# Held-back loads, a weight converted by halves, and eight-by-two diagonal blocks on another engine in a fused attention and feed-forward kernel

## The chip, the cores and the metric

One core of a Trainium2 chip runs the whole program. The metric is device time in microseconds (us); lower is better. TensorE (PE) multiplies, VectorE (DVE) and ScalarE (ACT) do elementwise work, GpSimd (POOL) does one kind of reduction and issues transfers, SyncE (SP) only issues transfers. Each engine works through its own queue in order.

## What is computed

```python
# q, k, v: 8 batches x 8 heads x 576 tokens x 64
q_s = softmax(q, over the 64 of a head)
k_s = softmax(k, over the 576 tokens)
kv  = einsum('bhsd,bhse->bhde', k_s, v)          # 64 x 64 for each batch and head
x   = einsum('bhsd,bhde->bhse', q_s, kv)         # -> 4608 tokens x 512
h   = x @ w_in                                   # 512 -> 2048
x   = maximum(0.01 * h, h) @ w_out               # 2048 -> 512
h   = max(x @ w1, x @ w2, x @ w3)                # 512 -> 768, three times
out = h @ w_out2                                 # 768 -> 512
```

The inputs are 64-bit floats for the weights (read as pairs of 32-bit words) and every matmul operand is split into a high and a low part, so that a product takes three matmuls (hi·hi, hi·lo, lo·hi).

## The kernel before, in words

The 4608 tokens are nine chunks of 512. A chunk is first put through the attention and then, transposed, through the first feed-forward layer, whose 2048 hidden columns are 16 blocks (m = 0 to 15); each block has a weight tile (its piece of `w_in` and of `w_out`). The list `TURNS` says in which order chunks 0 and 1 take the blocks while the weights come in: chunk 0 with block 0, chunk 1 with blocks 0 and 1, chunk 0 with blocks 1 to 3, and so on. A step of this loop is one projection (12 matmuls, `project`), the leaky function, a split (`split_g`) and the second product of the step before (12 matmuls, `a_out`).

A planner (the framework's scheduler, with a simulated timeline) orders each engine's instructions when the program is built. It takes what is ready first, and of what is ready the instruction that stands earlier in the program; `pin` ties an instruction behind the one written before it on its engine. So the order of the instructions may change anywhere when something is edited.

The part around the change is the start, before the loop is in its rhythm.

- `first_units(0)` and `first_units(1)` are the attention units of chunks 0 and 1: four pairs of heads, each with a k unit (`kv_unit`, L382) and a q unit (`q_unit`, L500), advanced stage by stage by `advance` (L787). Their k, v and q are loaded by SP into one `spare` tile for each pair (L396, L399, L505).
- The k unit transposes k (L411), takes the maximum (L416 to L418), the exponential (L430, L431, L428), multiplies by v (L455), and writes the two 64x64 diagonal blocks of kv, scaled, into `plain`: a ScalarE copy from PSUM (L465), after two small VectorE instructions (L460, L461).
- The q unit subtracts, exponentiates, sums and scales (L526 to L549), transposes on TensorE (L555) and copies the transpose out of PSUM into a tile `qf` (L557), for which there are three buffers for four pairs of heads; then it multiplies with `plain` (L563) and splits the result (`split_x`: L605 to L615), which is the operand of `project`.
- PSUM has four buffers under the name `ps`, which the transposes, the kv products and the products of L563 take in turn.
- Chunk 2's units are background work of the loop, planned for steps 13 to 21 (`plan_units`, L724); they load through POOL (L396, L445, L505) into tiles of a small pool (two buffers for k and q, one for v). `behind_step` (L366) makes a tile's first column depend on the newest result of the loop, by a ScalarE copy of one column.
- `conv_a(m, after)` (L720) converts the 64-bit weight m into the high and low part by `split_words` (L155): ScalarE takes the absolute value of the whole tile into a single-buffered tile `ca` (L172), VectorE makes seven passes over 1024 columns (L173 to L185), ScalarE writes the high part (L177) and a copy that goes to DRAM (L188, L189). Weight 0 is converted before the loop, weights 1 and 2 in step 0 (L923, L924), the others at the steps in `BEGUN`, two steps after their load (`load_a`).

## Time and profile before

| what | value |
|---|---|
| median of 3 runs | 1414.36 us (1412.64 to 1415.6) |
| the profiled execution | 1412.0 us; its span from first to last instruction 1410.2 us |
| PE busy | 1382.3 us, 98% of the span |
| DVE, ACT, POOL busy | 866.5, 673.7, 157.5 us |
| granted TensorE clock, mean | 0.997 |

All times in the rows are microseconds from the start of the span. An instruction's row gives its start and its duration, and in brackets how long its engine sat idle before it and what ended that. Where a row stands for several instructions (x4), the start is that of the first. Instructions of one engine overlap a little, so the distance between two starts may be shorter than a duration.

### The profile page before, as it was taken

How to read it: one execution, taken by the hardware profiler on the slowest of the kernel's cores; microseconds unless marked ns; L12 is line 12 of the kernel's file. 1: busy time of each engine (PE TensorE's matmuls, PEld its weight loads, DVE VectorE, ACT ScalarE, POOL GpSimd, SP SyncE). 2: the span in 40 equal slices, each digit the busy share in tenths (PEclk: the TensorE clock that was granted, in tenths of full speed). 3: DMA queues.
4: the chain of work that ended last, by engine and by line, in shares of the span. 5: the costliest groups of instructions: out<-in, count | busy, mean ns of one | idle time of the engine just before them, and what ended most of it. 6: DMA issues, size and time to landing. Idle time of an engine off the chain costs nothing.

```text
span 1410.2 us, 18328 instructions
## 1 busy us (share of the span) xinstructions
PE 1382.3 (98%) x6624; PEld 1128.3 (80%) x6624; DVE 866.5 (61%) x1500; ACT 673.7 (48%) x1382; POOL 157.5 (11%) x261
## 2 busy tenths in 40 slices
PE   6999998999999999999999999999999999999998
PEld 4688777788888788888887888888888888888887
DVE  8878888865686794756756545766357255434311
ACT  6756867854675755654444444224224223322211
POOL 1000112210111120210222300011000000000000
PEclk9999999999999999999999999999999999999999
DMA  9478776743986956768698897765574573454601
GB/s 370 152 261 288 254 249 211 231 147 116 355 290 230 397 189 228 282 237 341 215 331 303 297 390 263 250 225 172 199 285 142 209 291 119 155 233 157 229 33 38
DMA packets 90826, 330.10 MB, mean 234 GB/s; under 512 B 10672, under 2 KB 27056, under 8 KB 67568
## 3 DMA queue, kind: packets, MB, share of 16 engines
q1 hardware_dynamic: 68512, 251.46, 49.4%
q0 software_dynamic: 19056, 66.98, 14.1%
q10 hardware_dynamic: 3168, 10.49, 1.9%
q8 instruction: 52, 0.85, 0.2%
q14 instruction: 38, 0.31, 0.1%
HBM read 253.66 MB, written 75.24 MB: 233 GB/s over the span
## 4 chain that ended last, share of the span: by engine, by line
PE 87%; DVE 5%; DMA 4%; ACT 3%; issue 2%; SPq 0%; ACTq 0%; DVEq 0%
PE ps L859 40%; PE acc L631 32%; PE ps L631 11%; DMA outw<-stream_out 1%; PE ps L455 1%; PE ps L583 1%; DMA stream_in<-room 1%; PE ps L563 1%; DMA spare<-in_q_dram 1%; DVE glo L652 1%; DMA room<-wi 0%; DMA lone<-room 0%; DVE side L824 0%; ACT qo L519 0%; DVE qsm L541 0%
## 5 line engine op out<-in xcount | busy, mean ns | idle before, releaser
L859 PE MATMUL ps<-op,group 128*128 128x512 f32 x1512 | 352.2, 389 | 0.0
L859 PEld LDWEIGHTS ps<-op,group 128*128 128x128 f32 x1512 | 283.8, 188 | 59.0 <-ACT snap L1091 0.2
L631 PE MATMUL acc<-ghi,outw 128*128 128x512 f32 x768 | 248.0, 391 | 1.9 <-ACT ghi L651 1.6
L859 PE MATMUL ps<-opA,group 128*128 128x512 f32 x1008 | 247.5, 391 | 1.1 <-ACT opA L819 0.6
L859 PEld LDWEIGHTS ps<-opA,group 128*128 128x128 f32 x1008 | 188.1, 188 | 41.6 <-ACT snap L987 1.4
L631 PEld LDWEIGHTS acc<-ghi,outw 128*128 128x128 f32 x768 | 143.6, 188 | 33.5 <-ACT ghi L651 3.1
L631 PE MATMUL acc<-glo,outw 128*128 128x512 f32 x384 | 150.4, 392 | 0.5 <-DVE glo L652 0.2
L631 PE MATMUL acc<-wo,h 128*128 128x512 f32 x558 | 135.6, 389 | 0.0
L631 PE MATMUL acc<-ghi,w 128*128 128x512 f32 x384 | 127.1, 395 | 0.9 <-ACT ghi L651 0.9
L631 PE MATMUL ps<-xhi,w 128*128 128x512 f32 x384 | 125.7, 394 | 1.0 <-ACT g L909 0.8
L1091 ACT ACTIVATE snap<-ps 128x512 f32<-128x512 f32 x108 | 61.9, 597 | 135.4 <-PE ps L859 135.1
L631 PEld LDWEIGHTS acc<-wo,h 128*128 128x128 f32 x558 | 104.8, 188 | 21.7
L652 DVE TENSOR_TENSOR glo<-g,ghi 128x512 fp32r<-128x512 f32 x102 | 69.9, 691 | 59.8 <-ACT ghi L651 59.3
L1106 DVE TENSOR_TENSOR snap<-snap,ps 128x512 f32<-128x512 f32 x72 | 49.1, 684 | 93.2 <-ACT snap L1091 69.8
L651 ACT ACTIVATE ghi<-g 128x512 fp32r<-128x512 f32 x102 | 63.6, 630 | 46.9 <-DVE g L1291 27.3
L631 PEld LDWEIGHTS ps<-xhi,w 128*128 128x128 f32 x384 | 72.1, 188 | 17.3 <-ACT g L909 1.2
L631 PEld LDWEIGHTS acc<-glo,outw 128*128 128x128 f32 x384 | 72.1, 188 | 17.2 <-DVE glo L652 2.5
L631 PEld LDWEIGHTS acc<-ghi,w 128*128 128x128 f32 x384 | 71.5, 188 | 16.8 <-ACT ghi L651 1.5
L1102 DVE TENSOR_TENSOR best<-snap,ps 128x512 f32<-128x512 f32 x36 | 24.7, 686 | 87.9 <-PE ps L859 37.7
L631 PE MATMUL acc<-glo,w 128*128 128x512 f32 x192 | 75.2, 392 | 0.5 <-DVE glo L652 0.5
L631 PE MATMUL ps<-xlo,w 128*128 128x512 f32 x192 | 75.1, 391 | 0.1
L1115 ACT ACTIVATE h<-best 128x512 fp32r<-128x512 f32 x48 | 30.3, 631 | 87.3 <-DVE best L1108 86.9
(185 smaller groups left out, 1915.6 us busy)
## 6 DMA issues: line engine op xcount, KB each, us to landing
group<-stream SPq DMA_DIRECT2D x62, 1024.0 KB, 6.2
outw<-stream_out SPq DMA_DIRECT2D x48, 1024.0 KB, 8.1
group<-stream_in SPq DMA_DIRECT2D x42, 1024.0 KB, 7.5
stream<-room POOLq DMA_DIRECT2D x66, 256.0 KB, 6.3
raw<-in_wa_dram SPq DMA_DIRECT2D x16, 1024.0 KB, 7.0
x<-st SPq DMA_DIRECT2D x40, 256.0 KB, 3.7
room<-in_wb_dram POOLq DMA_DIRECT2D x18, 512.0 KB, 6.2
stream_out<-w SPq DMA_DIRECT2D x16, 512.0 KB, 3.6
```

The source lines that it names most:

```text
L455: nc.tensor.matmul(acc[z, : D + 1], lhsT=ke[:, r, z], rhs=vt[:, r, h], start=r == 0, stop=r == RK - 1)
L563: nc.tensor.matmul(both(xps, c0, c1), lhsT=plain_of(b, hp), rhs=halves(qf, c0, c1), start=True, stop=True)
L583: nc.tensor.matmul(both(xps, c0, c1), lhsT=a, rhs=halves(y, c0, c1), start=i == 0, stop=i == 2)
L631: nc.tensor.matmul(acc, lhsT=l, rhs=r, start=first and i == 0, stop=last and i == 2)
L651: nc.scalar.activation(hi[:, z], g[:, z], AF.Copy)
L652: nc.vector.tensor_tensor(lo[:, z], g[:, z], hi[:, z].bitcast(F32), op=ALU.subtract)
L859: nc.tensor.matmul(bank, lhsT=l, rhs=r, start=fresh and first, stop=last, skip_group_check=not fresh)
L1091: nc.scalar.activation(t, bank, AF.Copy)
L1102: nc.vector.tensor_tensor(g, snap, bank, op=ALU.add)
L1106: nc.vector.tensor_tensor(snap, snap, bank, op=ALU.add)
L1115: nc.scalar.activation(h[:, m, 0], g, AF.Copy)
```

## The change

It has four parts. In chunk 2, the loads of k for the first two pairs of heads, of q for the same two and of v for the first are put behind a `behind_step`, so that they can't be issued before the step in which they are written. The conversion of weight 1 is a generator with three parts: the absolute value right after step 0's split, the first half of the columns (`w_in`'s piece) once all k units of chunk 1 are done, the second half after the rest of chunk 1's attention; each VectorE and ScalarE pass is over 512 columns instead of 1024. For chunks 0 and 1 the diagonal blocks of `plain` are written by VectorE. And for these chunks the transposed q goes back into the tile that q came from, instead of one of three `qf` buffers.

```diff
+    def split_by_halves(raw, hi, lo, keep):
+
+        words = raw.bitcast(U32).rearrange("p (n t) -> p n t", t=2)
+        a = cp.tile([P, 2 * N], U32, tag="ca", name="ca")
+        pin(nc.scalar.activation(a.bitcast(F32), words[:, :, 1].bitcast(F32), AF.Abs))
+        yield
+        for i in range(2):
+            z = slice(i * N, i * N + N)
+            au, high, low = a[:, z], words[:, z, 1], words[:, z, 0]
+            af, bf = au.bitcast(F32), high.bitcast(F32)
+            pin(nc.vector.tensor_scalar(af, af, MOST_HIGH, LEAST_HIGH, op0=ALU.min, op1=ALU.max))
+            nc.vector.tensor_scalar(au, au, 3, 0x3FFFFFF8, op0=ALU.logical_shift_left, op1=ALU.bitwise_and)
+            nc.vector.scalar_tensor_tensor(au, high, 0xC0000000, au, op0=ALU.bitwise_and, op1=ALU.bitwise_or)
+            nc.scalar.activation(hi[:, z], af, AF.Copy)
+            nc.vector.tensor_scalar(high, au, 0xFF800000, None, op0=ALU.bitwise_and)
+            nc.vector.scalar_tensor_tensor(bf, low, 2.0**-52, bf, op0=ALU.mult, op1=ALU.mult)
+            nc.vector.tensor_tensor(af, af, bf, op=ALU.add)
+            nc.vector.tensor_tensor(lo[:, z], af, hi[:, z].bitcast(F32), op=ALU.subtract)
+            yield
+        copy = raw.bitcast(F32)[:, :N]
+        nc.scalar.activation(copy, a.bitcast(F32)[:, :N], AF.Copy)
+        pin(nc.scalar.dma_start(keep, copy))
...
         fetch = nc.sync if b < FIRST else nc.gpsimd
+        if b == FIRST and hp < 2:
+            behind_step(ke[:, 0, 0:1])
         fetch.dma_start(ke, k[b, hp])
...
+            if b == FIRST and hp == 0:
+                behind_step(vt[:, 0, 0, 0:1])
             fetch.dma_start(vt, v[b, hp])
...
-                nc.scalar.activation(plain_of(b, hp)[z, z], acc[z, :D], AF.Copy, scale=rc[z])
+                if b < FIRST:
+                    nc.vector.tensor_scalar(plain_of(b, hp)[z, z], acc[z, :D], rc[z], None, op0=ALU.mult)
+                else:
+                    nc.scalar.activation(plain_of(b, hp)[z, z], acc[z, :D], AF.Copy, scale=rc[z])
...
+        if c == FIRST and hp < 2:
+            behind_step(qt[:, 0:1])
         (nc.sync if c < FIRST else nc.gpsimd).dma_start(qt, q[c, hp])
...
-        qf = ap.tile([P, N], F32, tag=("qf", "qhi", "qlo")[hp % 3] if early else "qf", name="qf", bufs=1)
+        if c < FIRST:
+            qf = qt
+        else:
+            qf = ap.tile([P, N], F32, tag=("qf", "qhi", "qlo")[hp % 3] if early else "qf", name="qf", bufs=1)
...
     def conv_a(m, after):
         tiles[m] = weights(words.pop(m), after, whole_in[m])
+        wA[m] = parts(tiles[m])
+
+    def conv_by_halves(m):
+        raw = words.pop(m)
+        if raw.dtype != I64:
+            yield
+            yield
+            tiles[m] = weights(raw, None, whole_in[m])
+        else:
+            w = tiles[m] = wp.tile([P, 2, 2, N], F32R, tag="w", name="w")
+            yield from split_by_halves(raw, flat(w[:, 0]), flat(w[:, 1]), whole_in[m])
         wA[m] = parts(tiles[m])
...
             newest["g"] = g
+            if step == 0:
+                convert = conv_by_halves(1)
+                next(convert)
             background(step)
             if prev is not None:
                 a_out(*prev)
...
                 second = advance(second, 2)
                 a_out(*prev, hold=True)
                 prev = None
+                while len(done) < 2 * NP:
+                    second = advance(second, 1)
+                next(convert)
                 advance(second)
+                for _ in convert:
+                    pass
                 for f in range(KDM):
                     store(f, x2[turn][:, f], accs[c][f], busy=True)
-                conv_a(1, spare(1, NP - 1))
                 conv_a(2, x_tiles(1)[0][:, NP - 1].bitcast(F32))
```

## Rows read from the trace of the kernel before

**Rows 1.** The page's first part: busy time, share of the span and instructions of each engine.

```profile
PE 1382.3 (98%) x6624; PEld 1128.3 (80%) x6624; DVE 866.5 (61%) x1500; ACT 673.7 (48%) x1382; POOL 157.5 (11%) x261
```

**Rows 2.** One of TensorE's waits, whole run: for what, us in total, times, longest.

```profile
PE ps L455 <- DMA vt<-in_v_dram: 2.3, 1, 2.3
```

**Rows 3.** Stretches: busy us (count) of PE, PEld, DVE, ACT, POOL; clock, DMA share, GB/s.

```profile
10.00:20.00 10.00, 6.76 (x32) 5.21 (x31) 8.68 (x26) 7.36 (x17) 0.00 (x0) 0.83 1.03 405
...
120.00:140.00 20.00, 20.00 (x90) 16.54 (x90) 18.35 (x25) 13.11 (x22) 1.48 (x1) 1.00 0.84 297
```

**Rows 4.** Transfers of 0 to 70 us issued by POOL: count, KB each, us to landing.

```profile
ke<-in_k_dram POOLq DMA_DIRECT2D x2, 320.0 KB, 7.6
qt<-in_q_dram POOLq DMA_DIRECT2D x2, 256.0 KB, 8.5
vt<-in_v_dram POOLq DMA_DIRECT2D x1, 325.0 KB, 9.1
```

**Rows 5.** The same view of 8.0 to 8.6 us: the load of weight 0.

```profile
raw<-in_wa_dram SPq DMA_DIRECT2D x1, 1024.0 KB, 11.8
```

**Rows 6.** The chain that ended last (start, us, what): chunk 0's last q; a later second product.

```profile
4.01 8.65 DMA spare<-in_q_dram
...
73.63 2.72 PE acc L631 x12
```

**Rows 7.** VectorE in order of time, 0 to 80 us: start, us, instruction.

```profile
7.25 0.69 DVE L526 TENSOR_REDUCE qmx<-spare 128x8 f32<-128x512 f32 x1 [0.99 <-DMA spare<-in_q_dram]
...
12.68 0.69 DVE L526 TENSOR_REDUCE qmx<-spare 128x8 f32<-128x512 f32 x1 [1.28 <-DMA spare<-in_q_dram]
...
22.07 0.69 DVE L173 TENSOR_SCALAR ca<-ca 128x1024 f32<-128x1024 f32 x1 [1.69 <-ACT ca L172]
...
33.96 0.69 DVE L541 TENSOR_REDUCE qsm<-spare 128x8 f32<-128x512 f32 x1 [0.57 <-ACT spare L539]
...
45.35 1.54 DVE L427 TENSOR_TENSOR spare<-spare,ps 128x640 f32<-128x640 f32 x2
```

**Rows 8.** ScalarE in order of time, 0 to 80 us.

```profile
14.00 0.63 ACT L539 ACTIVATE spare<-spare 128x512 f32<-128x512 f32 x1 [1.54 <-DVE spare L538]
...
20.88 1.16 ACT L172 ACTIVATE ca<-raw 128x1024 f32<-128x1024 f32 x1
...
25.88 1.94 ACT L465 ACTIVATE plain<-ps,rc 64x64 f32<-64x64 f32 x6
...
48.55 1.14 ACT L172 ACTIVATE ca<-raw 128x1024 f32<-128x1024 f32 x1
...
51.68 0.60 ACT L557 ACTIVATE qf<-ps 128x512 f32<-128x512 f32 x1
```

**Rows 9.** TensorE in order of time, 0 to 120 us.

```profile
46.37 2.79 PE L455 MATMUL ps<-spare 128*64 128x65 f32 x80
50.40 4.17 PE L563 MATMUL ps<-qf,plain 128*128 128x64 f32 x16 [1.25 <-ACT plain L465]
...
56.52 0.50 PE L631 MATMUL ps<-xhi,w 128*128 128x512 f32 x1 [0.22 <-DVE xlo L615]
...
58.12 0.86 PE L631 MATMUL ps<-xhi,w 128*128 128x512 f32 x3
```

**Rows 10.** Single lines: engine, instruction, count, ns min/median/max, first and last start, shape.

```profile
L465 ACT ACTIVATE plain<-ps,rc x24: 302/308/310, 23.7 to 193.2; 64x64 f32<-64x64 f32 x24
...
L474 DVE SCALAR_TENSOR_TENSOR kvlo<-ps,rc,kvhi x40: 231/284/293, 224.5 to 559.4; 64x64 fp32r<-64x64 f32 x40
...
L460 DVE TENSOR_SCALAR rc<-ps x32: 141/157/160, 22.7 to 558.0; 128x1 f32<-128x1 f32 x32
```

**Rows 11.** SyncE's queue: stores of converted weights 2 and 3, each issued when its weight is done.

```profile
68.28 0.36 SPq L688 DMA_DIRECT2D stream_out<-w  x1
...
78.14 0.37 SPq L688 DMA_DIRECT2D stream_out<-w  x1
```

**Rows 12.** POOL in order of time, 120 to 200 us: issue of a later load of chunk 2.

```profile
151.22 0.56 POOL L396 DMA_DIRECT2D ke<-in_k_dram  x1 [13.84 <-ACT qt L533]
```

## The prediction, made before the changed kernel was seen

> **What bounds the kernel now.** I read the page's busy times first: TensorE is busy 98% of the span [rows 1]. What is not busy, some 28 us, is the only time that this change can win, since it removes no matmul. The list of TensorE's waits and the view by stretches say where that lies: a good half in the first 60 us, nearly nothing between 60 and 200 us, and a few later waits, of which one for a v load is the longest (2.3 us [rows 2]). From about 57 us on TensorE goes through its list without a gap, 2.72 us for each half step of 12 matmuls [rows 6], so whatever comes earlier at that point comes off the end, one for one, as long as nothing behind it becomes late. The question is thus: by how much does the first projection of chunk 1 (56.52 us [rows 9]) come earlier?
>
> What leads up to it I read from the chain of waits and the engines' rows in order of time. Until about 20 us the loads end last: the DMA engines are full (share 1.03, 405 GB/s [rows 3]), chunk 0's last q lands at 4.01 + 8.65 = 12.66 us [rows 6], and VectorE stood 0.99 and 1.28 us for q loads [rows 7], ScalarE 1.54 us for the work behind the last [rows 8]. Weight 0 lands at about 8.05 + 11.8 = 19.9 us [rows 5]; its absolute value runs at 20.88 [rows 8], and VectorE stood 1.69 us for that [rows 7]. From 22 to 46.9 us (45.35 + 1.54 [rows 7]) VectorE works almost without a break: weight 0's seven passes, then both softmaxes of chunk 1. Only behind it does TensorE come into play again: 46.37 kv products, 1.25 us waiting for a diagonal block, 50.40 the products with q, 56.52 the projection [rows 9]. So there are two pieces to price: the shift of VectorE's end at 46.9 us, and what lies between that and the projection.
>
> **Part 1, the held loads.** Five transfers leave the start: 2 x 320 + 2 x 256 + 325 = 1477 KB, 1.51 MB [rows 4]; at 405 GB/s [rows 3] that is 3.7 us of full DMA engines. Some half to three quarters of it flows before 12.66 us, since the first of the five land 7.6 us after an issue at about 4 us [rows 4]; so the last q should land 1.9 to 2.8 us earlier, and weight 0 about 3.7 us earlier, at some 16 us. VectorE's own gain from this lies between 0.5 us (its order blocks it on something else) and all of 0.99 + 1.28 = 2.3; I take 1.5, by the wait of ScalarE, whose row carries the chain on [rows 8]. Then the wait of 1.69 us: it goes if the absolute value is placed earlier, and it is filled in any case if chunk 1's first q, which also lands 3.7 us earlier, is there for VectorE to work on. Between 0 and 1.7 I take 1.4, as there are two ways to fill it. Where the loads go: to steps 13 to 17, some 120 to 145 us, into a stretch whose DMA share is 0.84 [rows 3]; 1.51 MB at 297 GB/s more or less fill what is left there for 20 us. Each has two steps, about 11 us, between issue and use, against 7.6 to 9.1 us of landing in the crowded start [rows 4], so I cost that at nothing; if that cover is gone, a kv product waits for v as one does now, 2.3 us [rows 2]. The five ScalarE copies of one column cost some 0.2 us each where ScalarE has a third of its time free [rows 3]. On POOL's queue the held issues stand ahead of chunk 2's reductions; they are released by a step's result that comes before those, so nobody waits longer.
>
> The VectorE instructions of that stretch bear on this too: POOL's next load there took 0.56 us to issue with VectorE 92% busy [rows 3, 12]. The Trainium skill (SBUF — State Buffer, section "SBUF: two separate sides") warns that a DMA issued from GpSimd has its descriptors held up while VectorE runs in a two-port mode, which speaks against moving these five into the busy loop. By the row the move costs nothing, by the rule each could start later by a pass of VectorE, still inside its 11 us, so the sum would stay and only the chance of a late v grows.
>
> **Part 2, the diagonal blocks.** Sixteen ScalarE copies of 0.308 us [rows 10] become VectorE instructions. The trace has no such instruction. Its neighbours are the same operation on one column, 0.157 us, and a two-input one on the same block, 0.284 [rows 10]; I take 0.2, nearer to the first because successive instructions overlap. Eight of them fall in chunk 0, into VectorE's unbroken stretch: 8 x 0.2 = 1.6 us later (1.3 to 2.3). Chunk 0's own products with q start earlier (the other pairs' blocks stood behind the weight's high part on ScalarE until 25.88 [rows 8]), but VectorE does not wait for those, so I count nothing for it.
>
> So VectorE's end at 46.9 us moves by 1.5 + 1.4 - 1.6 = **1.3 us earlier** (ends: 0.5 + 0 - 2.3 = 1.8 later; 2.3 + 1.7 - 1.3 = 2.7 earlier).
>
> The Trainium skill (VectorE: DVE Perf Modes, section "Specifications") places VectorE nearer to SBUF and ScalarE nearer to PSUM, which speaks against moving a read of PSUM to VectorE. Here ScalarE's block takes 0.308 us and VectorE's larger two-input one 0.284 [rows 10]: the trace doesn't bear it out. By the rule alone a block would be no cheaper than 0.308, and the shift 0.4 instead of 1.3.
>
> **Part 3, between VectorE's end and the projection.** Now: 46.37 the kv products, 2.79 us; ScalarE breaks off its blocks for weight 1's absolute value (48.55, 1.14 us [rows 8]); the fourth transpose of q keeps a PSUM buffer until 51.68, since its copy needs a `qf` buffer [rows 8], and the products with q get their buffer 1.25 us late [rows 9]. After: the absolute value is done in step 0, the `qf` wait is gone, and VectorE writes a block right behind its own reciprocal. Then TensorE has no reason to stop: 46.37 + 2.79 + 4.17 (products with q [rows 9]) + about 1.9 (the four products with minus one, which lie between the products with q and the projection: 56.52 - 50.40 - 4.17) + 2.72 for the projection [rows 6] = 57.9 us. Now the projection's twelve matmuls end at 58.12 + 7 x 0.227 = 59.7. So up to 1.8 us; some wait of the first product and the last low part stays, and I take **1.4 us** (0.4 to 1.8).
>
> Weight 1's first half must be there for the second projection, one half step (2.72 us) after the first starts: VectorE starts it when the blocks are done, at about 50 us, and its seven passes of 512 columns take at most half of the 9.9 us between two weights [rows 11], so by 55 us; the projection needs it at 57.9. Its second half is needed only after four half steps. The split into halves adds seven instructions, at most 0.16 us each by the one-column row [rows 10], half of them behind the point that matters: nothing. Each of these numbers moves with VectorE's end.
>
> **Sum.** 1.3 + 1.4 = 2.7 us; and 0.4 of the 0.57 us for which VectorE stands at 33.96 behind a late exponential of ScalarE [rows 7], which is freed of 8 x 0.308 = 2.5 us of blocks ahead of it: 3.1 us. Against the profiled execution that is 1412.0 - 3.1 = 1408.9; that execution lies 2.4 us under the median of the runs shown, and against this the forecast is 1414.4 - 3.1 = **1411.3 us**, 0.22% faster. Its own range is 1409.5 to 1413.0.
>
> **The rivals.** (a) *The conversions become the bound.* Weights 2 and 3 are finished 9.9 us apart [rows 11], paced by one `ca` buffer and VectorE, and TensorE needs weight 3 soon after 76 us. If TensorE starts 1.4 us earlier relative to that pace, it may run dry there; against it speaks that the planner can put a projection of the other chunk ahead (2.72 us [rows 6]). Part 3 is then lost, and of the rest some: gain 1, 1413.4 us. (b) *VectorE is the bound of the start and gets more to do.* If the loads were not what held it (its waits turn up at the next operand instead) and a block costs 0.29 us, chunk 0 is 2.3 us later, chunk 1's eight blocks run 2.3 us behind one another and the first half starts behind them, which gives part 3 away; 1414.4 + 2.3 = 1416.7 us, **slower**. It decides from the point at which VectorE's last k addition ends later than 46.9 us. For it: VectorE's unbroken rows. Against it: 3.96 us of waits ahead of them. (c) *The new order also removes later waits.* TensorE loses 2.3 us to one v load of a later chunk [rows 2], where the plan has put its issue late; the plan is made anew, and this wait may go: 1414.4 - 3.1 - 2.3 = 1409.0 us. The same lottery can add as much. (d) *The change doesn't do what it says*: the loads are held, but the planner keeps the order of before and everything else lands as late: 1414.4.
>
> **How the numbers follow.** Forecast 0.55; (a) 0.17; (b) 0.09; (c) 0.12; (d) 0.07. 0.2% of the time is 2.8 us, about what a measurement of this kernel can tell from no change, so the bound for faster is 1411.5. Of the forecast's 0.55 some 0.35 lies below that, and (c): 0.47 faster. Slower than 1417.2 is about half of (b) and the bad side of the lottery: 0.08. The rest, 0.45, is the same. The range from 1407.6 to 1415.0 leaves out (b), the far ends of (c), and no more.
>
> **What would show it.** Right: no POOL load before 100 us; chunk 0's last q lands near 10 us; VectorE's waits at 7.25, 12.68 and 22.07 gone or short; its last k addition ends at 45 to 46 us; blocks of about 0.2 us; the first projection of chunk 1 at 53 to 54.5 us, with no wait of TensorE up to 120 us. Wrong: an unchanged end of VectorE's chain, waits of TensorE for a weight's low part (L185) at 70 to 100 us, or for a v of chunk 2 near 140 us.

## The result, and the profile after

The changed kernel takes 1422.4 us (median; 1421.4 to 1424.8) where the kernel before, run beside it, takes 1412.6 us. The ratio is 1.0067, with a 95% interval from 1.0056 to 1.0078: 9.5 us slower. The profiled execution has a span of 1423.0 us against 1410.2: at 1424.8 us it is the slowest of the six, so the rows below show some 3 us more than the medians do.

Busy times of the engines over the whole span, after:

```profile
PE 1387.0 (97%) x6624; PEld 1130.8 (79%) x6624; DVE 872.9 (61%) x1523; ACT 670.1 (47%) x1371; POOL 158.9 (11%) x261
```

TensorE is not busy for 36 us now, against 28 [rows 1]; the count of matmuls is the same, and they take 4.7 us more. Where the 8 us without work lie is read by stretches (the columns are those of rows 3). First the kernel before, then after:

```profile
60.00:100.00 40.00, 40.00 (x178) 32.91 (x177) 32.45 (x36) 23.47 (x40) 0.00 (x0) 1.00 0.71 251
...
150.00:200.00 50.00, 50.00 (x291) 40.16 (x290) 42.34 (x76) 40.58 (x122) 9.10 (x14) 1.00 0.82 276
200.00:250.00 50.00, 44.99 (x261) 34.93 (x260) 39.21 (x83) 32.33 (x83) 8.75 (x14) 1.00 0.63 200
```

```profile
60.00:100.00 40.00, 38.13 (x166) 30.33 (x165) 30.65 (x36) 23.98 (x39) 0.00 (x0) 1.00 0.65 222
...
150.00:200.00 50.00, 46.96 (x273) 36.33 (x272) 41.36 (x76) 41.30 (x130) 9.49 (x15) 1.00 0.81 274
200.00:250.00 50.00, 41.92 (x213) 31.68 (x212) 38.81 (x78) 29.25 (x67) 8.40 (x12) 0.93 0.62 204
```

The loss is not in the start, where the change was made (TensorE is busy 45.9 of the first 60 us, and 45.6 before), but at 60 to 100 us (1.9 us) and above all at 150 to 250 us (6.1 us, at a lower granted clock as well). The list of TensorE's waits, 57 to 400 us, names what is late. Two of its rows (us in total, times, longest):

```profile
PE ps L666 <- DVE w L185: 4.3, 3, 2.1
PE acc L666 <- ACT ghi L686: 2.2, 3, 1.3
```

L185 is the last pass of a weight's conversion: TensorE waits for weights. In the kernel before, this wait does not occur. It is 4.3 of the 7.0 us that TensorE has lost between 60 and 400 us; the rest is spread over waits for ScalarE and VectorE. So the second thing to read is when each weight is done, from SyncE's stores as in rows 11:

```profile
71.69 0.37 SPq L723 DMA_DIRECT2D stream_out<-w  x1
81.56 0.36 SPq L723 DMA_DIRECT2D stream_out<-w  x1
...
218.18 0.36 SPq L723 DMA_DIRECT2D stream_out<-w  x1
```

Weight 2 is done 3.4 us later than before (71.69 against 68.28 [rows 11]), and weight 15 is done at 218.18 against 209.46, 8.7 us later. In the kernel before:

```profile
209.46 0.36 SPq L688 DMA_DIRECT2D stream_out<-w  x1
```

After the change, TensorE's own rows show that it stood for weight 2 and for the last weight itself:

```profile
55.23 0.50 PE L666 MATMUL ps<-xhi,w 128*128 128x512 f32 x1 [0.87 <-DVE xlo L650]
...
71.72 0.73 PE L666 MATMUL ps<-xhi,w 128*128 128x512 f32 x2 [1.04 <-DVE w L185]
...
218.17 0.81 PE L666 MATMUL ps<-xhi,w 128*128 128x512 f32 x2 [2.13 <-DVE w L185]
```

The first of these rows is the first projection of chunk 1: 1.3 us earlier than before (56.52 [rows 9]). The start did get faster; the conversions got slower.

How much room the last weight had in the kernel before, TensorE's rows there show. After the change the first two matmuls of that projection (215.42 and 215.65) had run on the high part alone, ahead of the wait. In the kernel before, where the high part is written by 205.24, the projection is divided in the same way:

```profile
205.77 0.50 PE L631 MATMUL ps<-xhi,w 128*128 128x512 f32 x1 [0.76 <-ACT g L909]
...
210.07 0.61 PE L631 MATMUL ps<-xhi,w 128*128 128x512 f32 x2
```

Two matmuls run at 205.77 and 206.11, then a second product, and the rest starts at 210.07, 0.6 us behind the weight's store at 209.46. TensorE did not wait, and yet there was next to no slack. VectorE at the seam of start and conversions, after the change:

```profile
54.95 0.49 DVE L650 TENSOR_TENSOR xlo<-ps,xhi 128x64 fp32r<-128x64 f32 x3
56.13 0.22 DVE L650 TENSOR_TENSOR xlo<-ps,xhi 128x64 fp32r<-128x64 f32 x1 [0.69 <-ACT xlo L647]
56.27 0.42 DVE L201 TENSOR_SCALAR ca<-ca 128x512 f32<-128x512 f32 x1
...
59.90 0.69 DVE L208 TENSOR_TENSOR w<-ca,w 128x512 fp32r<-128x512 f32 x1
63.32 0.69 DVE L173 TENSOR_SCALAR ca<-ca 128x1024 f32<-128x1024 f32 x1 [2.73 <-ACT ca L172]
```

The second half of weight 1 (from L201 on) is tied behind the last low part of chunk 1 (56.13) and ends at 60.6. Weight 2's first pass (L173) follows at 63.32, since its absolute value needs the one `ca` tile that weight 1 holds until 60.6. In the kernel before weight 1 was done at 57.6 and that pass started at 59.88:

```profile
59.88 0.69 DVE L173 TENSOR_SCALAR ca<-ca 128x1024 f32<-128x1024 f32 x1 [1.88 <-ACT ca L172]
```

So 3.0 of the 3.4 us by which weight 2 is late are there when weight 1 ends.

The parts of the change that were meant for the start did what they say. POOL's first load:

```profile
131.34 0.69 POOL L421 DMA_DIRECT2D ke<-in_k_dram  x1 [127.81 <-ACT ke L395]
```

### The profile page after: what moved, and what is told of

Its sections match the earlier page's. It is cut to its first block, busy times and chain, and to the rows that moved or that the text cites. A ratio compares the mean times of both kernels' runs of the same rounds, so it can differ in the third digit from the quotient of the medians.

```text
span 1423.0 us, 18344 instructions
## 1 busy us (share of the span) xinstructions
PE 1387.0 (97%) x6624; PEld 1130.8 (79%) x6624; DVE 872.9 (61%) x1523; ACT 670.1 (47%) x1371; POOL 158.9 (11%) x261
## 4 chain that ended last, share of the span: by engine, by line
PE 84%; DVE 6%; DMA 3%; ACT 3%; issue 2%; POOL 0%; ACTq 0%; DVEq 0%; POOLq 0%
PE ps L905 38%; PE acc L666 32%; PE ps L666 12%; PE ps L618 1%; PE ps L482 1%; DMA room<-in_wb_dram 1%; DMA stream<-room 1%; DMA outw<-stream_out 1%; ACT st L696 0%; DVE glo L687 0%; DMA ke<-in_k_dram 0%; DVE qsm L573 0%; ACT ghi L686 0%; DVE qmx L558 0%; DVE spare L570 0%
## 5 line engine op out<-in xcount | busy, mean ns | idle before, releaser
L1159 DVE TENSOR_TENSOR snap<-snap,ps 128x512 f32<-128x512 f32 x72 | 49.2, 685 | 93.5 <-ACT snap L1144 70.2
L686 ACT ACTIVATE ghi<-g 128x512 fp32r<-128x512 f32 x102 | 63.5, 629 | 43.2 <-DVE g L1344 27.3
```

Source lines behind the costliest of these rows:

```text
L686: nc.scalar.activation(hi[:, z], g[:, z], AF.Copy)
L1159: nc.vector.tensor_tensor(snap, snap, bank, op=ALU.add)
```

## The experiments

The first theory after reading these rows: the second half of weight 1 is late, weight 2 waits for it in the single `ca`, and the chain of conversions sets the end. Rivals: the held loads disturb the loop; the blocks on VectorE are dearer than thought; the transposes in place add waits. The times of the kernel before, beside these runs, were 1412.2 to 1413.1 us. For every kernel the profiled execution gives three moments: the first projection of chunk 1 (P), weight 2 done (W2), weight 15 done (W15), all in us. They are of one execution each and scatter by about a microsecond: n3, whose kernel differs from the one before only from weight 3 on, has P and W2 1.1 us earlier.

| kernel | P | W2 | W2 - P | W15 | W15 - W2 | median us | ratio to before, 95% |
|---|---|---|---|---|---|---|---|
| before | 56.5 | 68.3 | 11.8 | 209.5 | 141.2 | 1412.6 | |
| after | 55.2 | 71.7 | 16.5 | 218.2 | 146.5 | 1422.4 | 1.0056 to 1.0078 |
| e1_no_halves | 57.5 | 69.6 | 12.1 | 211.5 | 141.9 | 1414.9 | 1.0002 to 1.0026 |
| e2_no_hold | 59.5 | 76.0 | 16.5 | 222.4 | 146.4 | 1425.1 | 1.0066 to 1.0103 |
| e3_blocks_on_scalar | 51.1 | 67.3 | 16.2 | 214.1 | 146.8 | 1417.9 | 1.0018 to 1.0041 |
| e4_three_qf | 55.8 | 72.3 | 16.5 | 218.7 | 146.5 | 1422.1 | 1.0040 to 1.0078 |
| s1_hold_alone | 53.4 | 64.2 | 10.8 | 199.0 | 134.9 | 1410.1 | 0.9965 to 0.9989 |
| s2_halves_alone | 56.6 | 72.8 | 16.2 | 219.3 | 146.4 | 1424.1 | 1.0038 to 1.0079 |
| s3_blocks_alone | 57.9 | 70.2 | 12.3 | 211.3 | 141.1 | 1414.6 | 0.9997 to 1.0016 |
| m1_whole_in_place | 55.4 | 68.0 | 12.6 | 209.5 | 141.5 | 1412.8 | 0.9987 to 1.0006 |
| m2_second_half_untied | 54.8 | 66.5 | 11.7 | 208.4 | 141.9 | 1412.4 | 0.9990 to 1.0009 |
| m4_whole_scalar_blocks | 51.3 | 61.6 | 10.3 | 197.5 | 136.0 | 1408.9 | 0.9955 to 0.9979 |
| m5_hold_and_own_q | 53.4 | 63.5 | 10.1 | 200.3 | 136.8 | 1411.7 | 0.9982 to 1.0001 |
| m6_untied_scalar_blocks | 51.3 | 62.5 | 11.2 | 204.5 | 141.9 | 1408.7 | 0.9962 to 0.9983 |
| n1_absolute_first | 54.4 | 69.6 | 15.2 | 216.3 | 146.7 | 1420.3 | 1.0038 to 1.0068 |
| n2_both_halves_early | 54.8 | 68.9 | 14.1 | 216.4 | 147.5 | 1422.9 | 1.0043 to 1.0078 |
| n3_before_longer_conversions | 55.4 | 67.2 | 11.8 | 221.0 | 153.8 | 1423.3 | 1.0061 to 1.0095 |
| n4_best_longer_conversions | 51.6 | 61.8 | 10.3 | 215.3 | 153.5 | 1418.0 | 1.0023 to 1.0049 |
| n5_stores_behind | 54.5 | 71.0 | 16.5 | 212.4 | 141.4 | 1415.2 | 1.0010 to 1.0030 |
| n6_early_halves_stores_behind | 54.7 | 70.0 | 15.3 | 211.7 | 141.6 | 1413.1 | 0.9999 to 1.0021 |

### Undoing one part

**e1_no_halves**: weight 1 converted as before, in one piece in step 0, the rest as changed.

```diff
...
-                next(convert)
                 advance(second)
-                for _ in convert:
-                    pass
...
+                conv_a(1, spare(1, NP - 1))
                 conv_a(2, x_tiles(1)[0][:, NP - 1].bitcast(F32))
```

> The changed kernel with one part undone: weight 1 is converted as in the kernel before, whole and behind chunk 1's attention (the held loads, VectorE's diagonal blocks and the transposed q in its own tile stay). Changed kernel 1422.4, before 1412.6. Theory 1 (the pace of the weight conversions: in the changed kernel weight 1 is done at 60.7 instead of 57.7 us and weight 2 at 71.7 instead of 68.3, TensorE runs dry for weights and stays 10 us late): at most 1414, weight 2 done by 68.5, no wait of TensorE for a weight before 100 us. Theory 2 (the held loads crowd 130 to 200 us and weights 8 to 11 become late there): 1419, the first 3 us of the loss gone and the later 7 us still there. Theory 3 (any edit makes a new plan and the time scatters): anywhere from 1412 to 1425.

**e2_no_hold**: the three `behind_step` lines are gone.

```diff
-        if b == FIRST and hp < 2:
-            behind_step(ke[:, 0, 0:1])
...
```

> The changed kernel with one part undone: chunk 2's first loads are not held back. Theory 1 (conversion pace set by the conversion in halves): within 3 us of 1422, a little slower at the start because the 1.5 MB crowd the first 20 us again. Theory 2 (held loads): 1415, weights 8 to 11 no longer later than weights 2 to 6 are, and TensorE's waits of 140 to 240 us as in the kernel before. Theory 3 (scatter): anywhere from 1412 to 1425.

**e3_blocks_on_scalar**: the blocks are written by ScalarE again.

```diff
-                if b < FIRST:
-                    nc.vector.tensor_scalar(plain_of(b, hp)[z, z], acc[z, :D], rc[z], None, op0=ALU.mult)
-                else:
-                    nc.scalar.activation(plain_of(b, hp)[z, z], acc[z, :D], AF.Copy, scale=rc[z])
+                nc.scalar.activation(plain_of(b, hp)[z, z], acc[z, :D], AF.Copy, scale=rc[z])
```

> The changed kernel with one part undone: ScalarE writes the diagonal blocks of chunks 0 and 1 as before. In the changed kernel they cost VectorE 0.3 us each, 16 times. Theory 1: VectorE is 2.4 us freer in chunk 0 and its chain ends near 44 us; weight 1 is done some 2 to 4 us earlier, near 57 us, so 1417 to 1420. Theory 2: 1422 (the later loss stays, and the start gives 1 us at most). Theory 3: anywhere from 1412 to 1425.

**e4_three_qf**: the transposed q has its three buffers again.

```diff
-        if c < FIRST:
-            qf = qt
-        else:
-            qf = ap.tile(...)
+        qf = ap.tile(...)
```

> The changed kernel with one part undone: the transposed q of chunks 0 and 1 goes into one of three buffers for four pairs of heads, as before. Theories 1 and 2: within 2 us of 1422, the fourth product with q 1 us or so later. Theory 3: anywhere from 1412 to 1425.

Measured: without the halves 1414.9 us, 7.5 us less than the changed kernel; without the blocks on VectorE 1417.9, 4.5 less; without the held loads 1425.1, 2.7 more; with the old `qf` buffers 1422.1, the same. So the halves carry most of the loss, the blocks some, the held loads help, and the transposes in place do nothing that can be measured in the time. (By the first theory the kernel without the halves was to take at most 1414 us, with weight 2 done by 68.5; it took 1414.9, and weight 2 was done at 69.6.) The three that keep the halves have nearly the same interval from weight 2 to weight 15 (146.4 to 146.8 us), the one without them 141.9.

### One part alone

**s1_hold_alone** (the kernel before and the three `behind_step`), **s2_halves_alone** (and the conversion by halves), **s3_blocks_alone** (and VectorE's blocks). Their edits are the changed kernel's own:

```diff
+        if b == FIRST and hp < 2:
+            behind_step(ke[:, 0, 0:1])
...
```

> The kernel before with one part of the change: chunk 2's first loads held to their steps. Theory A (the chain of weight conversions is what the end hangs on: in six kernels so far the time stood as far from the kernel before as the store of weight 15; and the parts add up): 1410.2, that is 2.7 us faster, as taking this part out of the changed kernel cost 2.7; weight 1 done near 55 us, weight 15 near 207. Theory B (a new plan, the time scatters and parts do not add up): between 1408 and 1420 without relation to weight 1. My old theory 2 (held loads crowd the loop): above 1414.

```diff
...
+                next(convert)
                 advance(second)
+                for _ in convert:
+                    pass
...
-                conv_a(1, spare(1, NP - 1))
```

> The kernel before with one part: weight 1 converted by halves behind chunk 1's k units. Theory A: 1420.4, as taking this part out of the changed kernel gave 7.5 us; weight 15 some 7.5 us later than before's 209.5. Theory B: between 1410 and 1425, not near 1420. If halves hurt only because VectorE also has the diagonal blocks and the two collide: 1413 to 1415.

```diff
-                nc.scalar.activation(plain_of(b, hp)[z, z], acc[z, :D], AF.Copy, scale=rc[z])
+                    nc.vector.tensor_scalar(plain_of(b, hp)[z, z], acc[z, :D], rc[z], None, op0=ALU.mult)
```

> The kernel before with one part: VectorE writes the diagonal blocks of chunks 0 and 1. Theory A: 1417.4, as taking it out of the changed kernel gave 4.5 us; weight 1 done 4 to 5 us later. If the 0.3 us a block are paid only once, in chunk 0 (8 x 0.3): 1415.3. Theory B: between 1410 and 1425.

Measured: the held loads alone 1410.1 us, faster by 0.23% (0.11 to 0.35); the halves alone 1424.1, as slow as the whole change or slower; the blocks alone 1414.6, an interval that holds 1. By adding up what undoing each part had changed, 1410.2, 1420.4 and 1417.4 had been expected: the first came, the second lies inside its interval, the third did not come. What a part costs depends on what stands beside it: the blocks cost 1.6 us alone and gave back 4.5 when undone. Held loads bring weight 15 forward by 10.4 us (2.5 had been expected) and win 2.9: ahead of some 209 us the last weight is not what TensorE waits for. Later than that, it is: e1, s3, e3, n1, after, s2 and e2 line up, 1414.9, 1414.6, 1417.9, 1420.3, 1422.4, 1424.1 and 1425.1 us for W15 of 211.5, 211.3, 214.1, 216.3, 218.2, 219.3 and 222.4. The kernel before sat just at the bend, as its 0.6 us of slack say too. The line is good to some 2.5 us: n2, further down, lies that much above it.

### Halves, or their place

**m1_whole_in_place**: weight 1 converted whole, at the place of the first half. **m2_second_half_untied**: two halves, but the first VectorE pass of the second isn't tied behind the low parts.

```diff
-        for i in range(2):
-            z = slice(i * N, i * N + N)
+        for i in range(1):
+            z = slice(0, 2 * N)
```

> The changed kernel with weight 1 converted where it is now (absolute value in step 0, the rest right behind the k units of chunk 1) but whole, in seven passes of 1024 columns instead of fourteen of 512. If the splitting costs it (seven more instructions, some 1 us, and ScalarE's second high part to wait for): 1418 or less, weight 2 done below 70 us. If the place costs it (the passes stand ahead of chunk 1's split, and the plan of the loop behind it changes): 1422 or more, with the later conversions as late as in the changed kernel.

```diff
-            pin(nc.vector.tensor_scalar(af, af, MOST_HIGH, ...))
+            first = nc.vector.tensor_scalar(af, af, MOST_HIGH, ...)
+            if i == 0:
+                pin(first)
```

> The changed kernel with one edge removed: the first VectorE pass of weight 1's second half is no longer tied behind the VectorE instruction written before it, which is the last low part of chunk 1's split. Theory C (the splitting costs by this tie and by the order that the plan then takes: in the changed kernel VectorE waits 0.69 us at 56.1 for that low part, ScalarE then takes a result of the loop ahead of weight 2's absolute value, and from weight 2 to weight 15 the conversions need 146.5 us instead of 141.2): 1413 to 1415, weight 15 done near 210. Theory D (fourteen passes instead of seven are what costs): 1419 or more, weight 15 past 215.

Measured: 1412.8 and 1412.4 us; each of them alone takes back the whole loss. m2 still has its fourteen passes, so their number is not what costs. VectorE of m2 in order of time shows where the untied half went, and what held it in the changed kernel:

```profile
45.01 0.69 DVE L205 SCALAR_TENSOR_TENSOR ca<-raw,ca 128x512 uint32<-128x512 uint32 x1
45.61 0.81 DVE L454 TENSOR_TENSOR spare<-spare,ps 128x640 f32<-128x640 f32 x1
46.34 0.43 DVE L207 TENSOR_SCALAR raw<-ca 128x512 uint32<-128x512 uint32 x1
...
51.70 0.43 DVE L201 TENSOR_SCALAR ca<-ca 128x512 f32<-128x512 f32 x1
```

The passes from 45.01 to 50.2 us are the second half, put among the k additions and the blocks; the first half follows at 51.70. VectorE had room for it 10 us earlier than the tie allowed.

### The best of both

**m4_whole_scalar_blocks** is m1 with e3's edit, **m6_untied_scalar_blocks** m2 with e3's edit, **m5_hold_and_own_q** the kernel before with held loads and transposes in place.

```diff
...
+                nc.scalar.activation(plain_of(b, hp)[z, z], acc[z, :D], AF.Copy, scale=rc[z])
```

> Held loads, transposed q in its own tile, weight 1 converted whole behind chunk 1's k units with the absolute value in step 0, ScalarE writes the diagonal blocks. If the early conversion of weight 1 brings anything beside the held loads: below 1409.0. If TensorE is the bound once weight 15 is done before 205 us: 1409 to 1411, the same as the held loads alone (1410.1).

> The same, and ScalarE writes the diagonal blocks as before. Theory C: 1409 to 1411, since VectorE gets back 16 x 0.3 us; weight 15 before 206. Below that point TensorE is the bound (holding the loads alone brought weight 15 from 209.5 to 199 us and the time down by 2.9 only), so no less than 1407. Theory D: 1415 or more.

```diff
+        if c < FIRST:
+            qf = qt
...
```

> Held loads and the transposed q in its own tile, nothing else of the change. If the buffer of the fourth transposed q held up TensorE at 50 us, as my prediction had it: 1408.5 or less, the first projection of chunk 1 a microsecond earlier than with the held loads alone. If not (undoing this part of the changed kernel made no difference): 1410, as the held loads alone.

Measured: 1408.9, 1408.7 and 1411.7 us. The first two beat both kernels, the one before by 0.3% (0.17 to 0.45). Against the held loads alone (1410.1, 0.11 to 0.35% faster) the intervals overlap: that they win more is not shown. The third adds nothing to the held loads alone.

### Why the loop itself is slower

Open was why the interval from weight 2 to weight 15 is 146.5 us with the tied half and 141 to 142 without. **n1_absolute_first** ties a leaky function of ScalarE behind weight 2's absolute value, ahead of which it had slipped (61.68 us). **n2_both_halves_early** writes both halves ahead of the rest of the attention.

```diff
...
+            if step == 1:
+                tc.add_manual_dep(leak.ins, begun[-1].ins.name, tie, reason="order")
```

> The changed kernel, with the leaky function of the loop's step 1 tied behind the absolute value of weight 2 on ScalarE (in the changed kernel it runs between that conversion's one-column copy at 60.62 us and its absolute value at 62.17). Nothing else is tied. If this order on ScalarE makes the later plan slow: weight 2 done near 70 us, weight 15 at or below 212 us, 1416 us or less. If the cause is weight 1's second half itself (it ends at 60.6 us whatever ScalarE does after it): weight 2 at 70 to 71 us, weight 15 at 216 to 218, 1420 to 1422 us. A result of 1420 or more also says that 1.5 us of weight 2 is not worth more than 1.5 us of the time.

```diff
-                next(convert)
-                advance(second)
                 for _ in convert:
                     pass
+                advance(second)
```

> The changed kernel, with the second half of weight 1 written right behind the first, ahead of the rest of chunk 1's attention, so still two halves, fourteen passes and the same ties, only earlier. If what costs is that the second half stands behind chunk 1's last low part: weight 1 done near 56 us, weight 2 near 68, weight 15 near 209.5, 1413 to 1415 us (1412.8 with one conversion of the whole weight at this place, and up to 1.5 us more for seven further passes). If splitting into halves itself costs, wherever they run: 1418 us or more, weight 2 past 70 us.

Measured: 1420.3 and 1422.9 us (1418.1 to 1423.2). Both bring weight 2 forward, by 2.1 and 2.8 us (0.9 and 0.4 of it because the first projection comes earlier), and neither shortens the loop's interval (146.7 and 147.5). n2 was expected at 1413 to 1415 by the theory of the late place, so that theory explains only part. Its rival, that splitting costs wherever the halves run (1418 us or more), fits the time of n2 but not m2. In n2 weight 2 is done 0.6 us later than in the kernel before, and weight 15 nevertheless 7 us later. The rest had to be in the loop, and the list of VectorE's waits, 60 to 220 us, shows it: the first pass of a conversion waits for ScalarE's absolute value. Before, after, and n2:

```profile
DVE ca L173 <- ACT ca L172: 14.2, 11, 3.0
```

```profile
DVE ca L173 <- ACT ca L172: 24.9, 14, 3.2
```

```profile
DVE ca L173 <- ACT ca L172: 26.0, 14, 3.2
```

So 10.7 us more of waiting. It is more than the 5.3 us by which the interval grew, since it holds weight 2's own wait (2.73 us at 63.32; its like of before starts ahead of 60 us) and since VectorE did other work in some of these gaps before. From its absolute value to its store a conversion takes almost as long as before (128.1 us for thirteen weights against 127.4). ScalarE around weight 7, before and after, shows what it did instead (columns as in rows 8):

```profile
108.56 1.13 ACT L172 ACTIVATE ca<-raw 128x1024 f32<-128x1024 f32 x1
...
114.05 2.04 ACT L661 ACTIVATE st<-acc 128x512 f32<-128x512 f32 x4
```

```profile
111.98 1.09 ACT L696 ACTIVATE st<-acc 128x512 f32<-128x512 f32 x2 [0.37 <-PE acc L666]
112.95 0.20 ACT L171 ACTIVATE ca<-g 128x1 f32<-128x1 f32 x1
113.04 1.09 ACT L696 ACTIVATE st<-acc 128x512 f32<-128x512 f32 x2
114.00 1.15 ACT L172 ACTIVATE ca<-raw 128x1024 f32<-128x1024 f32 x1
```

At the end of each turn ScalarE copies four second products out of PSUM, 2.1 us. Before, these copies come 5 us behind the absolute value, while VectorE is in its passes. After, the plan puts the copies ahead of the absolute value, and VectorE stands. ScalarE even stood 0.37 us for the first product, with weight 6 done at 111.5 us, so it was not the order in which things came ready on the chip. That in the planner's own timeline the chain of conversions is late and the products are ready first is argued, not shown: that timeline is not on record. From one weight's end (its store) to the next absolute value, for weights 5, 7, 9, 11 and 13: 0.2, 0.2, 0.8, 0.8 and 3.2 us before, 1.6, 2.5, 2.9, 4.4 and 4.6 after. Over weights 3 to 15 these gaps add up to 13.8 us before and 18.4 after, 4.7 of the 5.3 us by which the interval grew.

**n3_before_longer_conversions** and **n4_best_longer_conversions** make the first pass of weights 3 to 15 twice, 13 x 0.69 = 9.0 us, in the kernel before and in m4.

```diff
...
+        if longer[0]:
+            nc.vector.tensor_scalar(af, af, MOST_HIGH, LEAST_HIGH, op0=ALU.min, op1=ALU.max)
```

> The kernel before, with the first VectorE pass of the conversion done twice for weights 3 to 15 (13 further passes of 1024 columns, 0.69 us each, 9.0 us in all; the second changes no value). Nothing in the start is touched. If the chain of conversions sets the end, and the kernel before has no slack in it: weight 15 done at 217 to 219 us instead of 209.5, 1420 to 1423 us. If VectorE's work in the loop is hidden behind TensorE: weight 15 later, but 1413 to 1415 us.

> The same 13 further passes in the version with held loads, weight 1 converted whole in its new place and ScalarE's blocks (1408.9 us, weight 15 at 197.5 us, some 12 us ahead of the kernel before). If the time follows weight 15 only when that comes after some 209 us: weight 15 at 205 to 207, 1409 to 1411 us, where the same passes cost the kernel before 8 to 10 us. If the passes cost because VectorE is busier in the loop, whatever weight 15 does: 1416 us or more.

Measured: 1423.3 us with W15 at 221.0 (11.6 later), and 1418.0 with W15 at 215.3. The first is the clean test of cause: the start is untouched, only conversions are longer, and the time follows the last weight nearly one for one (10.3 us for 11.6). The second missed: it was to show that 9 us are free where there are 12 us of slack, but the passes moved W15 by 17.8 us, past the bend. Its 1418.0 us fits the line of the others at 215.3, and it also fits the rival that was named for it, that VectorE's further passes cost whatever weight 15 does (1416 us or more); n4 does not tell the two apart. n5 below is free of it, as it changes no work of VectorE. The free side is shown by s1, m4 and m5 only. In n4 too VectorE's waits for the absolute value grow (7.3 us in m4, 16.7 in n4), but the gaps from a store to the next absolute value only from 10.5 to 12.2 us. Of the further 8.8 us 6.9 lie inside the conversions, and why was not tested.

**n5_stores_behind** is the changed kernel with the first of the four copies tied behind the absolute value, at six turn ends; **n6_early_halves_stores_behind** is n2 with the same tie.

```diff
...
-            nc.scalar.activation(st, acc, AF.Copy)
+            copy = nc.scalar.activation(st, acc, AF.Copy)
+            if busy and i == 0 and step in (3, 6, 10, 14, 18, 22):
+                tc.add_manual_dep(copy.ins, begun[-2 if step == 3 else -1].ins.name, tie, reason="order")
```

> The changed kernel, with one tie more at each of six turn ends: the first of the four ScalarE copies that take a finished second product out of PSUM (st<-acc, 2.1 us in all) stands behind the absolute value of the weight whose conversion is next there (weights 3, 5, 7, 9, 11 and 13). In the changed kernel these copies run between the end of one conversion and that absolute value, so that VectorE waits for them (1.6, 2.5, 2.9, 4.4 and 4.6 us from one weight's end to the absolute value of weights 5, 7, 9, 11 and 13); in the kernel before they mostly run while VectorE is in its passes (0.2, 0.2, 0.8, 0.8 and 3.2 us). If that is what makes the loop's conversions slower than before (146.5 us from weight 2 to weight 15 against 141.2): these gaps shrink to those of the kernel before, weight 15 done at 212 to 214 us, 1415 to 1418 us. If the gaps only go with something else: weight 15 at 217 or later, 1420 us or more, or TensorE waits for the copies instead.

> The same ties, with both halves of weight 1 converted ahead of the rest of chunk 1's attention (weight 2 done at 68.9 us there, against 71.7 in the changed kernel and 68.3 before). If the lateness of weight 2 and the copies in the gaps are together the whole loss: weight 15 done at 209 to 211 us, 1412.5 to 1415 us, so about the time before. If something else in the halves costs: 1418 us or more.

Measured: 1415.2 and 1413.1 us. The interval is back at 141.4 and 141.6, the gaps add up to 13.3 and 13.4. n5's waits of VectorE, 60 to 220 us, and its ScalarE around weight 5:

```profile
DVE ca L174 <- ACT ca L173: 16.0, 12, 2.7
```

```profile
90.46 1.14 ACT L173 ACTIVATE ca<-raw 128x1024 f32<-128x1024 f32 x1
91.50 0.59 ACT L959 ACTIVATE g<-ps 128x512 f32<-128x512 f32 x1
91.98 2.06 ACT L697 ACTIVATE st<-acc 128x512 f32<-128x512 f32 x4
```

With the halves, the blocks and the late weight 2 (71.0 us) all left as they are, moving these copies alone turns 0.67% slower into 0.20%: 6.6 of 9.5 us. With both halves early as well (n6) the interval holds 1, though weight 2 came at 70.0 us there and not at the 68.9 expected, and weight 15 only 0.7 us earlier than in n5. So the loss has two parts: a late second half that makes weight 2 late, and an order on ScalarE that makes the lateness grow at each turn's end. The second is the larger by n5, and n2 shows that it comes about without the first: there weight 2 is done almost as early as before, only TensorE is earlier. In all runs without the tie of n5 the slow interval (146.4 to 147.5 us) goes with W2 - P of 14.1 us and more, and the fast one with 12.6 and less (n3 and n4, with longer passes, aside). That this distance is what flips the plan is read from the table, not tested by itself. (In s1, m4 and m5, with 10.1 to 10.8 us, the interval is shorter still, 135 to 137 us.)

## Why the prediction was wrong, step by step

**What bounds the kernel.** "From about 57 us on TensorE goes through its list without a gap, ... so whatever comes earlier at that point comes off the end, one for one, as long as nothing behind it becomes late." The condition was named and not examined. The weight stores [rows 11] were read as a pace (9.9 us), not as a chain with an end: its last link at 209.46 us had 0.6 us of slack, and this could be seen by following the stores to weight 15 and TensorE's rows to 210.07. That the profile of before shows no wait for a weight (L185) was taken for slack.

**Part 1, held loads: right.** The waits at 7.25, 12.68 and 22.07 us [rows 7] are gone, weight 0's absolute value starts at 17.37 instead of 20.88 [rows 8], and alone the held loads bring VectorE's last k addition forward by 3.7 us (predicted: 1.5 + 1.4 = 2.9), the first projection by 3.2, and win 2.9 us. Moved to 131 us and later, they cost nothing that shows. The Trainium skill (SBUF — State Buffer, "SBUF: two separate sides") speaks of descriptors of GpSimd's loads held up while VectorE runs in a two-port mode; no run here shows it. Between 130 and 200 us, with VectorE 81% busy, POOL's loads took 4.3 to 4.9 us (medians by tile) to land, against 3.5 to 5.3 in the kernel before; the four issued up to 145 us took 5.6 to 7.0, inside the 11 us that the prediction gave them. (The 0.56 us issue that it set beside a VectorE 92% busy stands at 151.22 [rows 12], outside the stretch of that figure; from 150 to 200 us VectorE was 85% busy.)

**Part 2, the blocks: the term was mis-sized.** A block takes 0.29 us, the upper bound, not 0.2:

```profile
28.38 1.19 DVE L493 TENSOR_SCALAR plain<-ps,rc 64x64 f32<-64x64 f32 x4
```

And with the halves all sixteen stand on the path, not eight: chunk 1's come ahead of weight 1's first half on VectorE. 16 x 0.29 = 4.6 us; giving them back to ScalarE brings the first projection from 55.2 to 51.1 (and from 54.8 in m2 to 51.3 in m6). The prediction took 1.6. In the kernel before the blocks alone cost the first projection only 1.4 us (56.5 to 57.9, s3). It chose the price by the one-column row, though the row with the same block size (0.284 [rows 10]) was the nearer neighbour. The Trainium skill (VectorE: DVE Perf Modes, "Specifications") has VectorE sit closer to SBUF and ScalarE closer to PSUM. The prediction had worked out a price of 0.308 or more from that; the measured 0.29 lies just under it, nearer to it than to 0.2.

**Part 3: the step that failed.** "Its second half is needed only after four half steps. The split into halves adds seven instructions, ... half of them behind the point that matters: nothing." TensorE needed it no sooner, that held: no wait for its last pass (L208) stands in the list. But the next weight did: weight 2's absolute value waits for `ca`, and so the second half, tied behind the last low part, became the head of the conversion chain. Three things came of it: weight 2 is 3.4 us late (with the tie gone, m2, the whole loss is gone); ScalarE's copies fall into the gaps, 5.3 us more by weight 15 (with them moved back, n5, 6.6 of the 9.5 us are gone); and, as the chain had 0.6 us of slack, weight 15's 8.7 us came off the end. The seven instructions were put at 0.16 us each and sized well by that: the 14 passes sum to 2 x (3 x 0.43 + 4 x 0.69) = 8.1 us against 3 x 0.69 + 4 x 1.23 = 7.0 of the whole weight. The first half was done at 54.9 us, as forecast (55).

**The start as a whole.** VectorE's last k addition ended at 46.2 us (predicted 45 to 46), the first projection started at 55.2 (predicted 53 to 54.5). So the two pieces of its sum came to 0.7 us (forecast 1.3) and 0.6 (forecast 1.4; from the kv products' start to the projection, 9.5 us against 10.15). Part of the difference is that VectorE's very first instructions took 1.6 us longer in this one execution; in n1, n5 and n6 they did not, VectorE's last k addition ends at 45.4 to 45.5 and the projection comes at 54.4 to 54.7. There the first piece is 1.4 to 1.5 us, near the forecast by luck: held loads worth more than it took and blocks dearer than it took cancel. The base of the sum was high as well: 1414.4 us, where the kernel before took 1412.6 beside the changed one.

**The rivals.** (a) named the mechanism, conversions paced by one `ca` buffer become the bound, gave it 0.17, and priced it as a part of the gain lost (1413.4 us), because the planner could put another projection ahead. That lets TensorE fill a step now and then; it does not move the last weight. A chain that is itself made later can cost more than the whole gain, and the rival stopped at losing a part of it. (b), the only slower case, was tied to a block of 0.29 us, which came, and to VectorE's end past 46.9 us, which did not. (c) had TensorE's 2.3 us wait for a v load go: it is gone from the list, and a wait of 2.1 us ahead of another kv product (L482) stands in its place. The stated sign "waits for a weight's low part (L185)" is what the profile shows, three times: at 71.72, inside the stated 70 to 100 us, and at 208.65 and 218.17, far behind it.

## What to carry to other kernels

A queue of preparations that never makes the main engine wait may still have no slack: follow it to its last item and compare with the moment that item is needed, before costing anything that makes one of its items later at nothing. Ask of each piece that is postponed who holds its buffer next, not only who reads its result. And where a planner orders by readiness, a shift of two engines against each other can change an order far from the edit: look for work of one engine that sits in another's waiting gap, and tie it behind.

## What the hardware showed that was not expected

In this execution of the changed kernel TensorE's granted clock fell behind the new idle time (columns as in rows 3):

```profile
210.00:220.00 10.00, 6.52 (x25) 4.69 (x24) 8.86 (x13) 3.44 (x6) 1.52 (x1) 0.93 0.42 148
220.00:230.00 10.00, 8.59 (x43) 5.88 (x42) 5.20 (x10) 5.74 (x12) 0.56 (x1) 0.90 0.42 132
...
240.00:250.00 10.00, 7.91 (x61) 6.16 (x60) 8.95 (x25) 6.60 (x18) 3.72 (x6) 0.83 0.63 201
```

With TensorE busy 6.52 of 10 us the clock's mean is 0.93 of 2.4 GHz, then 0.90 and, at 240 to 250 us, 0.83: parts of these stretches ran at the lower level of 1.2 GHz. A matmul shows it, behind the wait for weight 14 and behind that for weight 15:

```profile
209.22 0.40 PE L666 MATMUL ps<-xlo,w 128*128 128x512 f32 x1
...
218.78 0.63 PE L666 MATMUL ps<-xlo,w 128*128 128x512 f32 x1
```

In the kernel before the same 50 us (200 to 250) have 3.1 us less idle time and a clock of 1.00. But it does not follow each time. In the profiled execution of e2, whose weight 15 is the latest of all, TensorE idles as long (it is busy 41.87 of these 50 us) and the clock stays:

```profile
220.00:230.00 10.00, 6.45 (x28) 4.58 (x26) 6.62 (x11) 4.55 (x8) 2.07 (x2) 1.00 0.54 187
```

So the clock can add to what a late weight costs, and the loss does not hang on it. And on VectorE a 64x64 block read from PSUM takes 0.29 us, nearly twice a single column (0.157 [rows 10]) and 0.94 of what ScalarE needs for it (0.308 [rows 10]).
